# Pooled attention and two feed-forward blocks on one core: one more pair of heads with its queries on partitions, column sums as two more columns, other ranks

## The chip, the cores and the metric

One core of a Trainium2 chip runs the whole program: TensorE (matrix products), VectorE, ScalarE, GpSimd, and SyncE, which here only issues DMAs. The metric is the time of one execution on the device in microseconds, the median of several runs. A profile is taken of one further execution.

## The reference

All arrays are float32. There are 4 batches of 8 heads, 1152 positions and 64 columns a head.

```python
q_pool = q.reshape(B, H, S // 2, 2, D).mean(axis=3)          # 576 queries a head
scores = matmul(q_pool, k.T) / sqrt(D)                       # 576 x 1152
scores = scores - max(scores, axis=-1)
attn = exp(scores); attn = attn / (sum(attn, axis=-1) + 1e-09)
x = heads side by side of matmul(attn, v)                    # 2304 x 512
h = maximum(x @ w_in, 0); g = s * (h * h) + b                # 2304 x 2048
y = g @ w_out                                                # 2304 x 512
gate = sigmoid(y @ w_gate); val = y @ w_val                  # 2304 x 1536
out = (gate * val) @ w_out2                                  # 2304 x 512
```

The weights are 64-bit floats that the kernel turns into 32-bit ones itself. In the first feed-forward block the shift `b` of `g` adds `b` times the column sums of `w_out` to `y`; the kernel computes these sums once, in batch 0's pass, and keeps them as a bias.

## The kernel before

**Number format.** A 32-bit operand is split into a high part in TensorE's fast 32-bit format and a low part, the remainder. A product of two such operands is three matmuls (high by high, high by low, low by high: `mm3`, L530 to L536, its matmuls on L532 to L534). Every split costs a cast (`copy_sb`, on ScalarE or GpSimd) and a subtraction (`tt_sb`, on VectorE or GpSimd, whichever the plan chooses).

**Attention.** Work goes by pairs of heads, four pairs a batch. `pair_prep` loads q, k and v, adds neighbouring queries, and transposes q and k by TensorE. Two forms of the rest exist.

- Keys on partitions (`pair_half`, batches 1 to 3): for each head and each half of the queries (288), nine blocks of 128 keys give scores with keys on partitions (two matmuls of 288 columns each, L762). ScalarE copies each block out of PSUM, VectorE keeps a running maximum over the blocks (L469), TensorE transposes it (L775), VectorE reduces it (L779), TensorE spreads it back to all partitions (L740), VectorE subtracts it (three tiles of 864 columns), ScalarE takes the exponential (L788), the result is split, and three P·V matmuls of 288 columns a block follow (L810, L811, L815). A column of ones beside V gives the sums; their reciprocal is taken either by a round trip through DRAM (`inverse`) or, where the pair ends a batch, directly (L859).
- Queries on partitions (`pair_rows`, batch 0): a block of 128 queries (eight full ones, and one that holds the last 64 of both heads) gets its scores in three PSUM banks of 384 keys (L893). VectorE takes the maximum along the row (L900, L903), and ScalarE the exponential straight out of PSUM with the maximum as bias, the row's sum falling out beside it (L907). P is then transposed by TensorE, 128 x 128 at a time (L938, and L940 for the half block), copied and split, and multiplied with V (L960). The transposed P has its high and low part in a `g` tile, which batch 0's attention shares with the feed-forward pass that follows.

**First feed-forward block** (`ffn1`, once a batch): `x` is split, 16 tiles of hidden columns are computed ("up", two halves of 288 tokens), squared, split into a `g` tile (high part, low part), and every four of them are multiplied with `w_out` ("down") into four output tiles. In batch 0, ahead of the second half of each output tile, eight matmuls of two columns (L623: two high and low weight tiles by four hidden tiles, against a tile of ones) add up the column sums of `w_out`. Batch 0's pass also decodes the weights (L490 to L500) and stores them to DRAM; later passes fetch them back. The pass of a batch needs `x` of all four pairs; it runs beside the next batch's attention.

**Second feed-forward block** (`ffn2`): twice, each for two batches, after all attention; batch 3's first pass stands between.

**What sets the order.** The kernel records every operation with its engine (or two to choose from), an estimated duration, what it reads and writes, and a rank; `Plan.order` then plays these through time, and at each step starts on every free engine the ready operation of lowest rank (class of work, plus an offset per name from `MOVED`, then position in the program, with a second offset). The order that results is written into each engine's queue and stays fixed. Tiles and PSUM banks are handed out by the same play, with the numbers in `ROOM`: 8 banks in all; at most 8 for tag `pr` (batch 0's attention), 4 for `ps` (the other batches'), 6 for `ff`; six `pp` tiles and four `g` tiles.

The operations of "down" and the column sums:

```python
py = bank(fp)
for i in range(CH):
    mm3(f"{fp} down", lambda py=py: py.t[:, :HQ], HQ, ...)
if b == hf == 0:
    def column_sums(py=py, w2=w2, ds_=ds_):
        for i in range(CH):
            for w in range(2):
                nc.tensor.matmul(py.t[:, HQ:HQ + 2], lhsT=w2[i].t[:, w, ds_], rhs=ones2, ...)
```

Of the kernel before, what the change touches and what calls it, by code (L numbers as in the profile page):

```python
# [32 lines left out]
DIRECT = (1, 2)  # L33
BANKS = {"pr", "ps", "pm", "acc", "ff", "p2"}
# [4 lines left out]
    "q load": (32, -5),  # L39
    "k load": (33.5, 3),  # L40
    "v load": (45.5, -117),
    "v hi": (-38, -97),
    "v lo": (2, -108),
    "q add": (0, -82),
    "q twice": (19, 27),
    "pr qT": (0, 101),
    "pr q hi False": (5, -93),
    "pr q lo False": (20, 103),
    "pr q hi True": (12, 120),
    "pr q lo True": (-8, -119),  # L50
    "pr kT": (-18.5, -55),
    "pr k hi": (-5, -44),
    "pr k lo": (-10, -71),
    "s b load": (30, -129),
    "r qk 1": (0, 189),
    "r max": (33.5, -59),
    "r - max": (-40, 91),
    "r exp": (57, -26),
    "r pT": (-40, 55),
    "r p": (-4.5, 57),  # L60
    "r p hi": (1, -106),
    "r p lo": (-40, -100),
    "r pv": (-40, -109),
    "r pT hi": (0, 83),
    "r pT lo": (36.5, 15),
    "r o": (-40, -167),
    "r x add": (35.5, -40),
    "r qk 2": (-17.5, 92),
    "r sums": (-34, 21),
    "r sums eps": (3.5, 149),  # L70
    "r 1 / sums": (0, -9),
    "r spread": (-40, -44),
    "r rows": (0, -88),
    "r rows mid": (0, 279),
    "r x / sums": (-1.5, -118),
    "r x / sums mid": (52, -15),
    "r end": (0, 96),
    "ps qT": (2, -29),
    "ps q hi False": (60, 90),
    "ps q lo False": (-37, -29),  # L80
    "ps kT": (-37.5, 16),
    "ps k hi": (23.5, 77),
    "ps k lo": (0, 7),
    "xx hi": (38, -89),
    "xx lo": (0, 93),
    "w load": (-1, -143),
    "w top": (-18.5, 97),
    "w scale": (-8, 23),
    "w low": (-19, 3),
    "w join": (11, 15),  # L90
    "w sign": (-36.5, 3),
    "w hi": (-40, 67),
    "w lo": (-40, 124),
    "w keep": (1, -49),
    "ff xx up": (59, 10),
    "ff relu": (-16, -95),
    "square": (-2.5, -142),
    "g hi": (7.5, 83),
    "g lo": (0, -7),
    "ff down": (52.5, 72),  # L100
    "column sums": (60, 35),
    "column sum": (30, 111),
    "ff y": (5, 96),
    "ff y add": (16.5, -46),
    "bias": (-10, -34),
    "y bias": (60, 105),
    "y store": (-21, -30),
    "qk": (33, -11),
    "s copy": (21, 43),
    "s max": (14, 112),  # L110
    "max T": (29, -81),
    "max": (60, 64),
    "max rows": (24.5, -22),
    "s - max": (16, 71),
    "exp": (1, 151),
    "p hi": (-40, 84),
    "p lo": (6.5, -89),
    "pv hi": (15, -72),
    "pv lo": (36, -18),
    "sums": (31.5, -144),  # L120
    "x": (44, 118),
    "sums out": (1, -73),
    "sums in": (3, 38),
    "1 / sums spread": (6.5, 129),
    "1 / sums out": (56, 107),
    "1 / sums in": (22, -4),
    "x / sums": (0, 61),
    "1 / sums": (46.5, -68),
    "w fetch": (-5.5, 3),
    "w come": (-40, 82),  # L130
    "x store": (28, 26),
    "yy load": (35.5, -43),
    "yy hi": (-5.5, -14),
    "yy lo": (0, 48),
    "p2 yy up": (51, -50),
    "gate": (22, 37),
    "gate val": (-40, 130),
    "h hi": (-4.5, -101),
    "h lo": (-36.5, 79),
    "down 2": (-16, -101),  # L140
    "out": (0.5, 5),
    "out add": (1.5, -9),
    "out store": (0, 9),
    "xx load": (1.5, -33),
    "p2 xx up": (23, -29),
    "p2 relu": (8, -42),
    "p2 down": (33.5, 24),
    "p2 y": (1.5, 110),
    "p2 y add": (60, 59),
# [196 lines left out]
def kernel(  # L346
# [47 lines left out]
    ones = const.tile([P, 1], F32, name="ones")  # L394
    nc.gpsimd.memset(ones, 1.0)
    zero = const.tile([P, 1], F32, name="zero")
    nc.gpsimd.memset(zero, 0.0)
# [3 lines left out]
    eps = const.tile([P, 1], F32, name="eps")  # L401
    nc.gpsimd.memset(eps, 1e-9)
    ones2 = const.tile([P, 2], F32R, name="ones2")
    nc.vector.tensor_copy(out=ones2, in_=ones.to_broadcast([P, 2]))
# [3 lines left out]
    s_sb = const.tile([P, 1], F32, name="s_sb")  # L408
# [169 lines left out]
    def ffn1(b, xx):  # L578
# [7 lines left out]
        for f0 in range(0, F1, CH):  # L586
            g = []
            for f in range(f0, f0 + CH):
# [4 lines left out]
                if b == B - 1 and f % 2:  # L593
                    gg = slot("fh", "h", [P, 2, 2 * SQ], F32R, lambda t: t[:, :, :SQ])
                else:
                    gg = slot("fg", "g", [P, 2, SQ], F32R)
# [7 lines left out]
                split_g(gg, lambda gg=gg: gg.t[:, 0], lambda gg=gg: gg.t[:, 1], lambda r=r: r.t, SQ, both, (gg, 0), (gg, 1))  # L604
                g.append(gg)
            w2 = [h for f in range(f0, f0 + CH, 2) for h in load_w((w_out, rows, "1d", f), (w_out, rows, "1d", f + 1))]
            for d in range(KC):
                ds_ = slice(d * P, (d + 1) * P)
                for hf in range(2):
                    cs = slice(hf * HQ, (hf + 1) * HQ)  # L610
                    py = bank(fp)
                    for i in range(CH):
                        mm3(
                            f"{fp} down", lambda py=py: py.t[:, :HQ], HQ,
                            lambda i=i, w2=w2, ds_=ds_: w2[i].t[:, 0, ds_], lambda i=i, w2=w2, ds_=ds_: w2[i].t[:, 1, ds_],
                            lambda i=i, g=g, cs=cs: g[i].t[:, 0, cs], lambda i=i, g=g, cs=cs: g[i].t[:, 1, cs],
                            [py, *((s, w) for s in (*w2, *g) for w in range(2))], i == 0, i == CH - 1, [y],
                        )
                    if b == hf == 0:
                        def column_sums(py=py, w2=w2, ds_=ds_):  # L620
                            for i in range(CH):
                                for w in range(2):
                                    nc.tensor.matmul(py.t[:, HQ:HQ + 2], lhsT=w2[i].t[:, w, ds_], rhs=ones2,  # L623
                                                     start=(i == w == 0), stop=(i == CH - 1 and w == 1))

                        pe("column sums", 2 * CH * mm(2), column_sums, [(s, w) for s in w2 for w in range(2)], [py], FP)
# [6 lines left out]
                    if f0 == 0:  # L633
                        act(f"{fp} y", HQ + 112, lambda d=d, cs=cs, py=py: nc.scalar.activation(  # L634
# [504 lines left out]
```

## Time and profile before

| | |
|---|---|
| runs | 1453.57, 1455.32, 1452.1 us (median 1453.57) |
| the profiled execution | 1461.99 us, its span 1460.2 us, mean granted TensorE clock 0.988 |
| TensorE busy | 1395.9 us (96%), 9292 matmuls |
| VectorE busy | 1076.8 us (74%) |
| ScalarE busy | 944.8 us (65%) |
| GpSimd busy | 763.7 us (52%) |
| column sums (L623) | 128 matmuls |
| HBM | 114 GB/s over the span |

The span reaches from the first to the last instruction; the execution's own time is a little longer. Matmuls overlap in the trace, so the duration of one is longer than its share of TensorE's time: two starts in a row tell the share. Batch 0's attention ends at 192 us, batch 1's at 460, batch 3's at 843, and from there on only feed-forward work is left. A granted clock of 1.00 is 2.4 GHz, and one of 0.5 is 1.2 GHz; a mean in between says how much of a stretch was at either.

### The profile page before, as it was taken

The page shows a single profiled execution, that of the slowest core. Times are in us where ns is not written, and L with a number is a line of the kernel's source. Part 1 is how long each engine was busy: PE and PEld are TensorE (multiplying, and loading weights), DVE is VectorE, ACT ScalarE, POOL GpSimd, SP SyncE. Part 2 cuts the span into 40 slices and gives each one's busy share as a digit, 9 for nine tenths or more (in the row PEclk, how much of TensorE's full clock was granted, in tenths as well). Part 3 has the DMA queues.
Part 4 walks back from the last instruction along what each step waited for, and adds up shares of the span by engine and source line. Part 5 has one row for each costly group of instructions (what it writes and reads, how often), then busy time and mean ns, then how long its engine had stood idle before and what let it go on. Part 6 is the DMA issues. An engine that isn't in the chain of part 4 may idle for free. (4 is left out here: it accounts for less than half of the span.)

```text
span 1460.2 us, 25288 instructions
## 1 busy us (share of the span) xinstructions
PE 1395.9 (96%) x9292; PEld 1332.2 (91%) x9292; DVE 1076.8 (74%) x1775; ACT 944.8 (65%) x2008; POOL 763.7 (52%) x650
## 2 busy tenths in 40 slices
PE   7988999998999999999999999999999999999998
PEld 6877889898889999999999999999898999989897
DVE  6889898998988888989999746737485126838562
ACT  6889888878788999898899735434142534534240
POOL 3677566778777565565766534525253003625230
PEclk9999999999999999999999999999999999999999
DMA  3335133444540533234241373312236544313112
GB/s 90 93 114 191 38 98 99 142 147 138 175 159 14 201 107 105 82 111 132 74 145 46 108 272 130 101 58 87 73 100 208 184 173 142 119 45 127 36 68 65
DMA packets 103044, 167.90 MB, mean 115 GB/s; under 512 B 44652, under 2 KB 80264, under 8 KB 93832
## 3 DMA queue, kind: packets, MB, share of 16 engines
q1 hardware_dynamic: 96008, 115.95, 25.5%
q0 software_dynamic: 6912, 50.33, 9.6%
q8 instruction: 73, 1.20, 0.3%
q14 instruction: 51, 0.42, 0.1%
HBM read 139.99 MB, written 26.28 MB: 114 GB/s over the span
## 5 line engine op out<-in xcount | busy, mean ns | idle before, releaser
L466 POOL TENSOR_TENSOR pp<-st,pp 128x864 fp32r<-128x864 f32 x94 | 202.5, 2161 | 33.8 <-ACT pp L456 27.8
L534 PE MATMUL banks<-yy,w 128*128 128x384 f32 x576 | 192.6, 334 | 0.3 <-POOL w L466 0.3
L533 PE MATMUL banks<-yy,w 128*128 128x384 f32 x576 | 192.6, 334 | 0.1
L532 PE MATMUL banks<-yy,w 128*128 128x384 f32 x576 | 192.5, 334 | 0.0
L463 ACT COPY st<-banks 128x288 f32<-128x288 f32 x432 | 153.9, 408 | 47.9 <-PE banks L762 43.6
L762 PE MATMUL banks<-qT,kT 128*128 128x288 f32 x864 | 165.7, 307 | 3.6 <-DVE mx L469 2.5
L469 DVE TENSOR_TENSOR mx<-banks,mx 128x288 f32<-128x288 f32 x336 | 150.6, 449 | 15.6 <-ACT st L463 8.1
L532 PE MATMUL banks<-xx,w 128*128 128x288 f32 x512 | 153.5, 300 | 5.0 <-DMA w<-d_1u_1u 5.0
L469 DVE TENSOR_TENSOR st<-st,banks 128x864 f32<-128x864 f32 x144 | 149.7, 1044 | 3.8 <-PE banks L740 3.0
L534 PE MATMUL banks<-xx,w 128*128 128x288 f32 x512 | 151.8, 296 | 0.0
L533 PE MATMUL banks<-xx,w 128*128 128x288 f32 x512 | 151.7, 296 | 0.0
L490 POOL TENSOR_SCALAR raw<-raw 128x512 f32<-128x512 f32 x99 | 78.4, 792 | 129.1 <-DMA raw<-in_moe_w_gate_dram 40.9
L532 PE MATMUL banks<-g,w 128*128 128x288 f32 x448 | 137.0, 306 | 0.9 <-ACT xy L634 0.6
L788 ACT ACTIVATE st<-st 128x864 f32<-128x864 f32 x144 | 132.7, 929 | 6.4 <-DVE st L469 5.8
L762 PEld LDWEIGHTS banks<-qT,kT 128*128 128x128 f32 x864 | 128.7, 191 | 8.2 <-DVE mx L469 5.3
L533 PE MATMUL banks<-g,w 128*128 128x288 f32 x448 | 133.1, 297 | 0.0
L534 PE MATMUL banks<-g,w 128*128 128x288 f32 x448 | 133.1, 297 | 0.0
L810 PE MATMUL banks<-pp,vt 128*128 128x288 f32 x432 | 122.3, 303 | 10.6 <-ACT pp L456 7.9
L493 ACT ACTIVATE raw<-raw 128x512 f32<-128x512 f32 x104 | 71.2, 686 | 79.5 <-POOL raw L490 73.3
L811 PE MATMUL banks<-pp,vt 128*64 128x288 f32 x432 | 119.5, 296 | 0.0
L466 POOL TENSOR_TENSOR w<-raw,w 128x512 fp32r<-128x512 f32 x64 | 100.3, 1569 | 19.8 <-ACT w L456 18.6
L494 DVE TENSOR_SCALAR raw<-raw 128x512 uint32<-128x512 uint32 x104 | 74.1, 715 | 47.2 <-DMA raw<-in_moe_w_val_dram 18.3
(151 smaller groups left out, 4016.5 us busy)
## 6 DMA issues: line engine op xcount, KB each, us to landing
w<-d_1u_1u POOLq DMA_DIRECT2D x24, 1024.0 KB, 6.2
w<-d_1d_1d POOLq DMA_DIRECT2D x24, 1024.0 KB, 6.2
raw<-in_moe_w_out_dram SPq DMA_DIRECT2D x40, 512.0 KB, 4.1
raw<-in_moe_w_gate_dram SPq DMA_DIRECT2D x24, 512.0 KB, 4.5
raw<-in_moe_w_val_dram SPq DMA_DIRECT2D x24, 512.0 KB, 3.9
qn<-in_q_dram SPq DMA_DIRECT2D x16, 576.0 KB, 4.2
kn<-in_k_dram SPq DMA_DIRECT2D x32, 288.0 KB, 4.4
vn<-in_v_dram SPq DMA_DIRECT2D x32, 288.0 KB, 2.9
```

What stands on the lines that cost most here:

```text
L463: act(name, n, lambda: nc.scalar.copy(out=out(), in_=in_()), r, w, rank, sbuf=False)
L466: shared(name, n, lambda e: ENGINE[e].tensor_tensor(out=out(), in0=in0(), in1=in1(), op=op), r, w, rank, 2.15)
L469: dve(name, n, lambda: nc.vector.tensor_tensor(out=out(), in0=in0(), in1=in1(), op=op), r, w, rank)
L490: shared("w top", 512, lambda e: ENGINE[e].tensor_scalar(out=words(1).bitcast(F32), in0=words(1).bitcast(F32), scalar1=F64_TOP, scalar2=-F ...
L494: dve("w low", 512, lambda: nc.vector.tensor_scalar(out=words(0), in0=words(0), scalar1=29, scalar2=None, op0=ALU.logical_shift_right,), [ ...
L532: nc.tensor.matmul(ps(), lhsT=whi(), rhs=xhi(), start=first, stop=False)
L533: nc.tensor.matmul(ps(), lhsT=whi(), rhs=xlo(), start=False, stop=False)
L534: nc.tensor.matmul(ps(), lhsT=wlo(), rhs=xhi(), start=False, stop=last)
L762: nc.tensor.matmul(ps.t[:, :HQ], lhsT=kT.t[:, c], rhs=qq[:, w, hf * HQ:(hf + 1) * HQ], start=(w == 0), stop=(w == 1))
L788: act("exp", 3 * HQ, lambda s=s: nc.scalar.activation(out=s.t, in_=s.t, func=AF.Exp), [], parts, AT)
L810: nc.tensor.matmul(acc.t[:, :HQ], lhsT=vt.t[:, 3 * i + c, D:], rhs=hi.t[:, c], start=(i == c == 0), stop=False)
L811: nc.tensor.matmul(acc.t[:D, :HQ], lhsT=vt.t[:, 3 * i + c, :D], rhs=hi.t[:, c], start=False, stop=False)
```

## The change

- Pair 3 of batch 1 is computed with queries on partitions, in the form that batch 0 has. Its PSUM banks come from the tag `ps`, and its transposed P from `pp` tiles, two to a unit, in place of a `g` tile. Its names begin with `t` and `pt` and so have ranks of their own.
- The column sums are no matmuls of their own. A `g` tile is 32 columns longer and holds its low part first, then the high part, then two columns of ones, which GpSimd writes each time in batch 0's pass ("one"). In the second half's products the two matmuls with the high part of `g` are 290 columns wide in place of 288, so the sums of the weights' high and low parts arrive beside the result.
- The constants share one tile, the tile of ones for the column sums goes, and one small tile is padded to 128 bytes.
- All offsets in `MOVED` are replaced.

```diff
+ROWS = {(0, hp) for hp in range(4)} | {(1, 3)}
 MOVED = {
...
 }
...
-    s_sb = const.tile([P, 1], F32, name="s_sb")
+    s_sb = const.tile([P, 32], F32, name="s_sb")[:, :1]
...
+    def g_slot():
+        return slot("fg", "g", [P, 2 * SQ + 32], F32R)
+    def part(gg, w):
+        return gg.t[:, :SQ] if w else gg.t[:, SQ:]
...
-    def mm3(name, ps, n, whi, wlo, xhi, xlo, reads, first, last, to):
+    def mm3(name, ps, n, whi, wlo, xhi, xlo, reads, first, last, to, ps_lo=None):
         def issue():
             nc.tensor.matmul(ps(), lhsT=whi(), rhs=xhi(), start=first, stop=False)
-            nc.tensor.matmul(ps(), lhsT=whi(), rhs=xlo(), start=False, stop=False)
+            nc.tensor.matmul((ps_lo or ps)(), lhsT=whi(), rhs=xlo(), start=False, stop=False)
             nc.tensor.matmul(ps(), lhsT=wlo(), rhs=xhi(), start=False, stop=last)
...
-                    gg = slot("fg", "g", [P, 2, SQ], F32R)
+                    gg = g_slot()
+                if b == 0:
+                    plan.add("one", "POOL", 150, lambda gg=gg: nc.gpsimd.tensor_scalar(
+                        out=gg.t[:, 2 * SQ:2 * SQ + 2], in0=ones.to_broadcast([P, 2]), scalar1=1.0, scalar2=0.0, op0=ALU.mult, op1=ALU.add),
+                             [], [(gg, "one")], FE)
...
+                    n = HQ + 2 if b == 0 and hf else HQ
+                    cs, ch = slice(hf * HQ, hf * HQ + n), slice(hf * HQ, (hf + 1) * HQ)
                     py = bank(fp)
                     for i in range(CH):
                         mm3(
-                            f"{fp} down", lambda py=py: py.t[:, :HQ], HQ,
+                            f"{fp} down", lambda py=py, n=n: py.t[:, :n], n,
...
-                    if b == hf == 0:
-                        def column_sums(py=py, w2=w2, ds_=ds_):
-                            for i in range(CH):
-                                for w in range(2):
-                                    nc.tensor.matmul(py.t[:, HQ:HQ + 2], lhsT=w2[i].t[:, w, ds_], rhs=ones2,
-                                                     start=(i == w == 0), stop=(i == CH - 1 and w == 1))
...
-        by_rows = b == 0
-        tag = "pr" if by_rows else "ps"
+        by_rows = (b, hp) in ROWS
+        tag = "pr" if b == 0 else "ps"
...
-    def pair_rows(hp, prep, x):
+    def pair_rows(b, hp, prep, x):
...
+        def parts2():
+            if b == 0:
+                t = g_slot()
+                return [(t, (t, w), lambda w=w: part(t, w)) for w in range(2)]
+            return [(t, t, lambda t=t: t.t) for t in (slot("pp", "pp", [P, 3 * HQ], F32R) for w in range(2))]
...
-        if b == 0:
-            steps = pair_rows(hp, prep, x0)
+        rows_now = (b, hp) in ROWS
+        if rows_now:
+            steps = pair_rows(b, hp, prep, xs[b])
             next(steps)
         else:
             pair_half(b, hp, 0, prep)
```

## Rows read from the trace of the kernel before

**Rows 1.** Stages: us; busy us (instructions) by engine; TensorE clock, DMA share, GB/s.
```profile
0.00:192.00 192.00, 165.25 (x1110) 149.26 (x1111) 158.80 (x353) 160.66 (x459) 117.44 (x138) 0.96 0.35 106
192.00:460.00 268.00, 249.04 (x1822) 239.86 (x1822) 241.18 (x398) 225.83 (x456) 197.06 (x136) 0.97 0.40 128
460.00:843.00 383.00, 374.74 (x2813) 363.33 (x2812) 334.56 (x551) 337.56 (x697) 230.44 (x169) 1.00 0.34 109
843.00:1460.20 617.20, 606.91 (x3554) 579.77 (x3552) 342.26 (x475) 220.72 (x397) 218.75 (x208) 0.99 0.35 116
```

**Rows 2.** TensorE's waits, 192 to 480 us: total us, times, longest.
```profile
PE banks L810 <- ACT pp L456: 6.4, 3, 3.9
PE banks L740 <- DVE mc L779: 3.4, 3, 2.0
```

**Rows 3.** Timeline of TensorE around one burst: start, us, instruction.
```profile
239.85 0.95 PE L623 MATMUL banks<-ones,w 128*128 128x2 f32 x8
240.66 0.38 PE L532 MATMUL banks<-g,w 128*128 128x288 f32 x1
240.88 0.30 PE L533 MATMUL banks<-g,w 128*128 128x288 f32 x1
```

**Rows 4.** Full stretches: 384-column matmuls alone, then 288-column ones (columns of rows 1).
```profile
1060.00:1080.00 20.00, 20.00 (x117) 20.00 (x116) 19.12 (x23) 9.19 (x17) 13.35 (x11) 1.00 0.32 101
1180.00:1200.00 20.00, 20.00 (x153) 20.00 (x152) 6.08 (x11) 5.93 (x11) 2.12 (x4) 1.00 0.60 211
```

**Rows 5.** Timeline of TensorE in a batch-0 pair (queries on partitions).
```profile
36.95 0.77 PE L960 MATMUL banks<-g,vt 128*128 128x320 f32 x4
37.56 0.38 PE L938 MATMUL banks<-ident,st 128*128 128x128 f32 x2
37.77 0.33 PE L940 MATMUL banks<-ident,st 128*128 128x64 f32 x2
37.95 0.39 PE L938 MATMUL banks<-ident,st 128*128 128x128 f32 x2
```

**Rows 6.** VectorE's groups by form: count | busy us, mean ns | idle before.
```profile
L469 DVE TENSOR_TENSOR mx<-banks,mx 128x288 f32<-128x288 f32 x336 | 150.6, 449 | 15.6 <-ACT st L463 8.1 <-PE banks L740 0.5
L469 DVE TENSOR_TENSOR st<-st,banks 128x864 f32<-128x864 f32 x144 | 149.7, 1044 | 3.8 <-PE banks L740 3.0 <-ACT st L463 0.7
L466 DVE TENSOR_TENSOR pp<-st,pp 128x864 fp32r<-128x864 f32 x50 | 66.3, 1327 | 13.2 <-ACT pp L456 12.2 <-POOL pp L458 0.9
L900 DVE TENSOR_REDUCE sg<-banks 128x1 f32<-128x384 f32 x108 | 56.4, 550 | 11.6 <-PE banks L893 11.0
L469 DVE TENSOR_TENSOR g<-banks,g 128x320 fp32r<-128x320 f32 x36 | 17.2, 482 | 4.2 <-ACT g L463 4.0
```

**Rows 7.** ScalarE's groups by form, the same columns.
```profile
L463 ACT COPY st<-banks 128x288 f32<-128x288 f32 x432 | 153.9, 408 | 47.9 <-PE banks L762 43.6 <-DVE mx L469 1.9 <-POOL xx L466 0.3
L788 ACT ACTIVATE st<-st 128x864 f32<-128x864 f32 x144 | 132.7, 929 | 6.4 <-DVE st L469 5.8
L907 ACT ACTIVATE st<-banks,sg 128x384 f32<-128x384 f32 x108 | 62.8, 597 | 10.0 <-DVE sg L903 9.8
L907 ACT ACTIVATION_READ_ACCUMULATOR st<-banks,sg 128x1 f32 x108 | 23.5, 218 | 0.0
```

**Rows 8.** A stretch with a lower mean clock (columns of rows 1).
```profile
340.00:360.00 20.00, 15.35 (x97) 14.77 (x96) 16.69 (x27) 17.55 (x32) 17.74 (x12) 0.83 0.46 163
```

**Rows 9.** Timelines of VectorE and GpSimd: x divided by its sums, where pairs end.
```profile
113.74 0.22 DVE L469 TENSOR_TENSOR xy<-xy,banks 64x64 f32<-64x64 f32 x1
163.52 0.44 DVE L469 TENSOR_TENSOR xy<-xy,banks 64x64 f32<-64x64 f32 x2
192.33 0.23 DVE L469 TENSOR_TENSOR xy<-xy,banks 64x64 f32<-64x64 f32 x1
421.81 0.80 POOL L466 TENSOR_TENSOR xy<-xy,rr 128x288 f32<-128x288 f32 x1
459.73 0.65 DVE L466 TENSOR_TENSOR xy<-xy,s 128x288 f32<-128x288 f32 x1
```

More of the change, by code (lines that the diff above doesn't have):

```diff
@@ L57 @@
[L57 to L149, printed above, removed]
+    "q load": (5, -16),
+    "k load": (33.5, 8),
+    "v load": (49, -85),
+    "v hi": (0, -33),
@@ new lines @@
+    "v lo": (60, 95),
+    "q add": (60, 14),
+    "pr qT": (0, -183),
+    "pr q hi False": (12.5, -90),
+    "pr q lo False": (-2, -114),
+    "pr q hi True": (20.5, -2),
+    "pr q lo True": (40.5, 49),
+    "pr kT": (-15, -30),
+    "pr k hi": (0, 74),
+    "pr k lo": (-24, -95),
+    "s b load": (0, 61),
+    "r qk 1": (0, 18),
+    "r max": (21, 114),
+    "r - max": (-27, 50),
+    "r exp": (30, 52),
+    "r pT": (-31.5, 90),
+    "r p": (-19.5, -22),
+    "r p hi": (0, 81),
+    "r p lo": (-2, -12),
@@ new lines @@
+    "r pv": (-40, -101),
+    "r pT hi": (0, -44),
+    "r pT lo": (47.5, 168),
+    "r o": (-11.5, -132),
+    "r x add": (32, -65),
+    "r qk 2": (-17.5, 0),
+    "r sums": (36, -32),
+    "r sums eps": (5, -38),
+    "r 1 / sums": (-30, -140),
+    "r spread": (-0.5, 78),
+    "r rows": (-12.5, 121),
+    "r rows mid": (0, 87),
+    "r x / sums": (-0.5, -61),
+    "r x / sums mid": (58, -115),
+    "r end": (1.5, -70),
+    "ps qT": (58.5, -62),
+    "ps q hi False": (46.5, 117),
+    "ps q lo False": (0, 49),
@@ new lines @@
+    "ps kT": (13, 8),
+    "ps k hi": (20, 44),
+    "ps k lo": (-4.5, 84),
+    "xx hi": (17, 66),
+    "xx lo": (56, -103),
+    "w load": (-17, -11),
+    "w top": (0, -72),
+    "w scale": (0, -38),
+    "w low": (-15, -53),
+    "w join": (4.5, -116),
+    "w sign": (-15, -93),
+    "w hi": (-40, 198),
+    "w lo": (-22.5, -114),
+    "w keep": (-8.5, -14),
+    "one": (-40, -113),
+    "ff xx up": (60, 22),
+    "ff relu": (-7.5, 64),
+    "square": (-7.5, 68),
+    "g hi": (2.5, 51),
+    "g lo": (0, 60),
@@ new lines @@
+    "ff down": (60, -8),
+    "ff y": (25, 46),
+    "column sum": (0, 119),
+    "ff y add": (12.5, 121),
+    "bias": (23.5, 47),
+    "y bias": (21, 39),
+    "y store": (-6, 1),
+    "qk": (26, -103),
+    "s copy": (12.5, -50),
+    "s max": (8.5, -24),
+    "max T": (25, -25),
+    "max": (22, -112),
+    "max rows": (0, 155),
+    "s - max": (12.5, 86),
+    "exp": (0, -79),
+    "p hi": (-29.5, -83),
+    "p lo": (0, -90),
+    "pv hi": (14.5, 75),
+    "pv lo": (55, 225),
+    "sums": (40.5, -43),
@@ new lines @@
+    "x": (25, 31),
+    "sums out": (-2, -94),
+    "sums in": (-13, 111),
+    "1 / sums spread": (0, -73),
+    "1 / sums out": (55, -125),
+    "1 / sums in": (-5, -53),
+    "x / sums": (0, 105),
+    "pt qT": (47, -118),
+    "pt q hi False": (0, 95),
+    "pt q lo False": (0.5, -49),
+    "pt q hi True": (-40, -60),
+    "pt q lo True": (-2, -74),
+    "pt kT": (-40, -90),
+    "pt k hi": (22.5, 106),
+    "pt k lo": (60, 47),
+    "t qk 1": (35, 2),
+    "t max": (25, 108),
+    "t - max": (0, 108),
@@ new lines @@
+    "t exp": (60, 115),
+    "t pT": (-14, 99),
+    "t p": (-16.5, 34),
+    "t p hi": (0, 106),
+    "t p lo": (0, -115),
+    "t pv": (-40, -142),
+    "t pT hi": (-40, 58),
+    "t pT lo": (32.5, 116),
+    "t o": (0, -43),
+    "t x add": (0, -19),
+    "t qk 2": (-13, -21),
+    "t sums": (0, -124),
+    "t sums eps": (-6.5, 95),
+    "t 1 / sums": (3, -34),
+    "t spread": (0, 48),
+    "t rows": (-34, 50),
+    "t rows mid": (-0.5, 20),
+    "t x / sums": (5, -88),
+    "t x / sums mid": (10, 20),
@@ new lines @@
+    "t end": (-5, 28),
+    "w fetch": (-32.5, -85),
+    "w come": (2, -29),
+    "1 / sums": (57, 6),
+    "x store": (-10, 37),
+    "turn": (0, 51),
+    "yy load": (0, -89),
+    "yy hi": (0, -25),
+    "yy lo": (1, -20),
+    "p2 yy up": (30.5, 31),
+    "gate": (5, 73),
+    "gate val": (-40, 106),
+    "h hi": (25.5, 79),
+    "h lo": (-40, -79),
+    "down 2": (-40, 1),
+    "out": (17, -42),
+    "out add": (-12.5, 20),
+    "out store": (-40, 28),
+    "xx load": (-14.5, 30),
+    "p2 xx up": (-3, 20),
@@ L150 @@
+    "p2 relu": (0, 109),
+    "p2 down": (12.5, 8),
+    "p2 y": (49.5, -42),
+    "p2 y add": (35.5, 68),
 }
@@ L393 @@
     make_identity(nc, ident)
[L394 to L397, printed above, removed]
+    values = const.tile([P, 3], F32, name="values")
+    ones, zero, eps = (values[:, i:i + 1] for i in range(3))
+    for t, value in ((ones, 1.0), (zero, 0.0), (eps, 1e-9)):
+        nc.gpsimd.memset(t, value)
     qm = const.tile([P, 2, 2, P], F32R, name="qm")
     nc.vector.tensor_copy(out=qm.rearrange("p j w c -> p (j w c)"), in_=zero.to_broadcast([P, 4 * P]))
[L401 to L404, printed above, removed]
     sums2 = const.tile([P, KC], F32, name="sums2")
     bias = const.tile([P, KC], F32, name="bias")
-    s_sb = const.tile([P, 1], F32, name="s_sb")
+    s_sb = const.tile([P, 32], F32, name="s_sb")[:, :1]
     b_sb = const.tile([P, 1], F32, name="b_sb")
```

117 lines of the change are left out of this document (51 added, 66 removed).

## The prediction

> **What bounds the kernel now.** I read the busy time of each engine by stage first [rows 1]. From 843 us to the end TensorE is busy 606.9 of 617.2 us and VectorE idles nearly half of the time: only fewer TensorE instructions shorten that part, and the change removes none there. In batches 2 and 3 (460 to 843 us) TensorE is busy 374.7 of 383. In batch 1 (192 to 460 us), where nearly all that the change removes and adds lies, three engines are close together: TensorE 249.0 of 268, VectorE 241.2 (90%), ScalarE 225.8 (84%), GpSimd 197.1. TensorE is first there, but 19 us of the stage it stands still, and the list of its waits, read second, names ScalarE and VectorE as the longest releasers, in front of a P·V product and of the transposed maxima [rows 2]. Batch 0 (up to 192 us) has no feed-forward work to fill with and lets TensorE idle 26.8 us.
>
> So a TensorE microsecond removed in batch 1 is worth close to a microsecond, provided that VectorE and ScalarE don't fall due instead; and the start and the seams depend on the order alone.
>
> **The change part by part.** Column sums. The timeline of TensorE shows a burst of eight two-column matmuls [rows 3]: the first starts at 239.85, the next operation at 240.66, so 0.81 us; that operation then takes 0.22 us to its successor, where a 288-column matmul takes 0.131 (153 in 20 us of full work [rows 4]), so 0.90 us counted to there. There are 4 blocks of 4 hidden tiles by 4 output tiles, 16 bursts: 13.0 to 14.4 us. I take 13.7. What is added: 64 products of half 1, in each two matmuls wider by 2 columns, 256 columns. From 0.171 us at 384 columns and 0.131 at 288 [rows 4] a column costs 0.42 ns: 0.1 us. Net -13.6 us on TensorE.
>
> Of this burst the Trainium skill would say otherwise: "TensorE: Matmul & The Clock Gate", section "Back-to-back issue gap", gives 1 to 64 columns about 60 cycles, 25 ns. By that rule 128 of them are an estimated 3.2 us, and the whole change would add TensorE work. The trace disagrees: eight in 0.81 us are 101 ns each. The same page's section on LDWEIGHTS gives a load of 128 columns 107 ns, which the trace supports; no run here shows which of the two sets the pace.
>
> The sixteen new two-column writes stand on GpSimd, which has 71 us free in batch 1 [rows 1]; they depend on nothing but a free tile. I count nothing. If the cover were gone, the second half of a "down" product would wait for its tile's write, behind one long GpSimd operation at most, and with it all that follows on TensorE. Wider or padded tiles (g by 128 bytes, s_sb to 128) I take at nothing too: g was 36 times 128 bytes and is 37 times; no row of the trace tells start addresses apart.
>
> The moved pair, on TensorE. Keys on partitions, as now: 72 score matmuls and 108 P·V matmuls of 288 columns, 180 x 0.131 = 23.6 us, and 24 transposes for the maxima, at most at the 0.105 us of a full-width one (two from 37.56 to 37.77 [rows 5]), 2.5: 26.1 us. Queries on partitions: 60 score matmuls of 384 columns, 60 x 0.171 = 10.3; 72 transposes of P at 0.105, 7.6; 36 half-width ones at 0.09 (two from 37.77 to 37.95 [rows 5]), 3.2; 36 P·V of 320 columns at 0.152 (four from 36.95 to 37.56 [rows 5]), 5.5; 36 of 256 columns at 0.131 - 32 x 0.42 ns = 0.118, 4.2; five for the sums, 0.5. Sum 31.3 us: the pair costs TensorE 5.2 us more (4 to 7 with the scatter of these pitches).
>
> On VectorE the same pair: now 32 x 0.449 for running maxima, 12 x 1.044 for subtracting them, and its share of the low parts, 12 x 50/144 x 1.327: 14.4 + 12.5 + 5.5 = 32.4 us. Then 27 x 0.550 and half of 10,368 columns of low parts at 482 ns per 320: 14.9 + 7.8 = 22.7 us [rows 6]. That is 9.7 less, 4% of its batch-1 load; the small rest (reciprocals, reductions, the halves' sum) is alike. On ScalarE: now 36 x 0.408 + 12 x 0.929 = 25.8 us of copies and exponentials; then 27 x (0.597 + 0.218) = 22.0 [rows 7], but half of P's columns are then copied out of PSUM before they are cast. I take ScalarE as unchanged, give or take 3 us. The division's trip through DRAM for this pair's first half goes; it isn't what TensorE waits for in [rows 2].
>
> Stalls. TensorE's waits for VectorE's maxima and for casts of P in [rows 2] are of a kind that this pair no longer has; it gets those of batch 0 (scores waiting for a PSUM bank until the exponential has read it), with four banks in place of eight. With feed-forward products as filler I put the net at -1 us; the sides are -5 and +3. One long wait costs more than itself: in 340 to 360 us, where 3.9 us of [rows 2] fall, the granted clock is 0.83 [rows 8], that is a third of the stretch at 1.2 in place of 2.4 GHz, some 3.4 us of work not done.
>
> The order. Every name's rank is replaced, so every queue is shuffled: SP's loads, GpSimd's weight fetches and the compute engines. The trace of before has no row for that. What can be won or lost is TensorE's idle time, 26.8 + 19.0 + 8.3 + 10.3 us [rows 1]; a third of the first two is 15 us. Either sign is open: 0, with 15 us on both sides and 6 as the usual size.
>
> Sum: -13.6 + 5.2 - 1 + 0 = -9.4 us. The profiled execution of before took 1461.99 us, 1.8 above its span; with the change 1452.6. The median of the runs stands 8.4 below the profiled execution (1453.57), so the forecast is 1444.2 us.
>
> **The rivals.** (a) The other side: the moved pair ends later, and TensorE starves. The next feed-forward pass needs all four pairs. Now pair 2 ends at 421.81 (plus 0.8) and pair 3 at 459.73 (plus 0.65), 38 us later [rows 9]; in batch 0 pairs in the new form end 49.8 and 28.8 us after one another (113.74, 163.52, 192.33 [rows 9]), there with eight banks and four more buffers for the transposed P, which this pair hasn't. If it takes 50 us, the next pass comes 12 us later, with nothing but one block's "down" products to fill; TensorE loses these 12 us and some 3.4 at the lower clock, against 9.4 won: +6, 1459.6 us. It decides from 47 us on (38 + 9.4). Against it: 28.8 us was possible, and in batch 0 the other engines had weights to decode at the same time.
>
> (b) TensorE's relief is not cashed. If batch 1 goes at the pace of ScalarE, which the change leaves as it is, removed matmuls only lengthen TensorE's waits. For it: the longest waits in [rows 2] are for ScalarE's casts. Against it: ScalarE has 42 us idle there, VectorE 27. Time 1453, between 1450.7 and 1456.4.
>
> (c) The order gains as well: 8 us of batch 0's 26.8 idle on top of the sum, 1436 us, down to 1428. For it: that stage's idle is the largest of all. Against it: there is no filler in it, and its first microseconds are waits for data.
>
> (d) Two-column matmuls cost little by themselves, and other work would fill the same slots. At 25 ns each, far below the row, 3.2 us go and 5.2 come, with the stall's -1: +1, 1454.6 us; it is the result by the rule of the Trainium skill named above, and the row of the burst speaks against it.
>
> **How the numbers follow.** Forecast 0.56 (its own range 1438 to 1450.5: the bounds of the pair and the stalls, and 6 us for the order), (a) 0.12, (b) 0.13, (c) 0.17, (d) 0.02. What this kernel's measurement can tell from no change is 0.2%, 2.9 us. Faster: forecast and (c), 0.73. Same: (b) and (d), 0.15. Slower: (a), 0.12. The range 1430 to 1457 takes in the forecast, (b), (d) and most of (c), and leaves out the far end of (c) and most of (a), somewhat under 0.2.
>
> **What would show it.** Right: no two-column matmuls by themselves; TensorE's busy time down by about 8 us, all of it between 192 and 480 us; VectorE down by 8 to 10; the division that closes batch 1, at 459.7 us now, 8 to 10 us earlier, and the rest shifted with it. (a) is seen in an x that closes batch 1 after 460 us and a TensorE wait ahead of the next pass's first product; (b) in a batch 1 as long as now with more waits for ScalarE; (c) in a batch 0 that ends before 185 us. I would be wrong if batch 1 shrank by much less than the removed matmuls, or if the new order opened waits after 843 us, where the old one has 10.3 us in all.

## The result and the profile after

The changed kernel takes 1475.57 us (median, 1471.25 to 1477.15) against 1454.44 for the one before beside it: ratio 1.0134 [1.0116, 1.0153] over the runs taken beside each other (the two medians alone would give 1.0145), so 1.3% slower, not 0.6% faster. Its profiled execution took 1474.67 us, its span 1472.9.

The stages, with the columns of [rows 1]:

```profile
0.00:192.00 192.00, 164.59 (x1113) 150.01 (x1114) 159.39 (x354) 160.80 (x461) 119.03 (x143) 0.96 0.36 107
192.00:460.00 268.00, 243.24 (x1732) 230.81 (x1731) 239.58 (x407) 221.25 (x478) 188.93 (x154) 0.97 0.42 137
460.00:843.00 383.00, 368.66 (x2751) 355.46 (x2751) 334.44 (x546) 336.07 (x698) 235.05 (x168) 1.00 0.30 98
843.00:1472.90 629.90, 615.53 (x3615) 588.34 (x3613) 344.35 (x478) 220.82 (x398) 225.12 (x212) 0.99 0.36 116
```

TensorE does have less to do: 9205 matmuls in place of 9292, and with each counted at the median step, from a start to the next one, of its line and form in the same trace, 1332.3 us in place of 1340.6. That is 8.3 us less, where the sum had 13.6 - 5.2 = 8.4. What grew is its idle time: in 192 to 460 us from 19.0 [rows 1] to 24.8, in 460 to 843 from 8.3 to 14.3, afterwards from 10.3 to 14.4. (A second profile of the kernel before, below, has 16.8, 8.3 and 8.6.) No burst of two columns is left, and the wider products are there (groups of TensorE by form):

```profile
L570 PE MATMUL banks<-g,w 128*128 128x290 f32 x64 | 19.8, 310 | 0.3 <-DVE kT L507 0.3
L572 PE MATMUL banks<-g,w 128*128 128x290 f32 x64 | 19.0, 296 | 0.0
```

Batch 0 ends as before, batch 1 two us later rather than nine earlier (VectorE's timeline, answering [rows 9]):

```profile
191.65 0.23 DVE L507 TENSOR_TENSOR xy<-xy,banks 64x64 f32<-64x64 f32 x1
...
461.70 0.23 DVE L507 TENSOR_TENSOR xy<-xy,banks 64x64 f32<-64x64 f32 x1
```

TensorE's waits from 192 to 480 us: the one for ScalarE's casts of P has shrunk from 6.4 us [rows 2] to 1.4, and several others stand in its place.

```profile
PE banks L780 <- DVE mc L819: 5.5, 5, 1.9
PE banks L815 <- DVE mx L507: 3.1, 3, 2.1
PE banks L855 <- POOL pp L504: 2.8, 3, 1.7
PE banks L1009 <- DVE pp L507: 2.2, 3, 1.5
PE banks L850 <- ACT pp L494: 1.4, 4, 0.5
```

VectorE's groups by form, answering [rows 6]. The pair's own saving is here: -12.4, -13.1 and -7.9 us in the first three rows, +13.5 in the fourth, +4.3 in the fifth and +3.1 in two more shapes of it, -12.5 in all. Yet VectorE's total went from 1076.8 to 1077.8 us: under the new order it took single operations that GpSimd had before (three additions of queries, and the like), and some operations took longer each (five of `x<-x,s` 1532 ns on the mean, where four took 934).

```profile
L507 DVE TENSOR_TENSOR mx<-banks,mx 128x288 f32<-128x288 f32 x308 | 138.2, 450 | 21.1 <-ACT st L501 11.5 <-PE banks L802 0.3
L507 DVE TENSOR_TENSOR st<-st,banks 128x864 f32<-128x864 f32 x132 | 136.6, 1042 | 2.6 <-PE banks L780 2.5
L504 DVE TENSOR_TENSOR pp<-st,pp 128x864 fp32r<-128x864 f32 x46 | 58.4, 1271 | 11.1 <-ACT pp L494 9.6 <-POOL pp L496 1.3
L942 DVE TENSOR_REDUCE sg<-banks 128x1 f32<-128x384 f32 x135 | 69.9, 549 | 13.6 <-PE banks L935 13.1
L507 DVE TENSOR_TENSOR pp<-banks,pp 128x320 fp32r<-128x320 f32 x9 | 4.3, 481 | 0.4 <-ACT pp L501 0.3
```

And the time behind the attention, where nothing was removed or added, is part of the loss. SyncE stores the last `x` of the attention at 842.9 us, and from there to the end of the span it takes 630.0 us; before it took 623.8 and, in a second profile of that kernel, 620.3. (There the last `x` is stored at 836.4 and 835.7 us, some 7 us ahead of the 843 at which [rows 1] is cut.)

### The profile page after: what moved, and what is told of

Read it like the earlier page. It is cut to its first block, busy times and chain, and to the rows that moved or that the text cites. A ratio compares the mean times of both kernels' runs of the same rounds, so it can differ in the third digit from the quotient of the medians.

```text
span 1472.9 us, 25105 instructions
## 1 busy us (share of the span) xinstructions
PE 1392.0 (95%) x9205; PEld 1324.6 (90%) x9205; DVE 1077.8 (73%) x1783; ACT 938.9 (64%) x2033; POOL 768.1 (52%) x675
## 4 chain that ended last, share of the span: by engine, by line
PE 60%; ACT 16%; DVE 10%; DMA 6%; issue 5%; POOL 2%; SPq 0%; DVEq 0%; ACTq 0%; POOLq 0%
PE banks L570 12%; PE banks L572 12%; PE banks L571 12%; PE banks L802 3%; ACT st L828 3%; ACT st L501 3%; PE banks L1090 3%; PE banks L1091 3%; PE banks L1089 3%; ACT pp L494 2%; DVE mx L507 2%; PE banks L935 2%; PE banks L1009 2%; PE banks L850 2%; PE banks L855 2%
## 5 line engine op out<-in xcount | busy, mean ns | idle before, releaser
L504 POOL TENSOR_TENSOR pp<-st,pp 128x864 fp32r<-128x864 f32 x86 | 185.5, 2165 | 39.8 <-ACT pp L494 31.7
L501 ACT COPY st<-banks 128x288 f32<-128x288 f32 x396 | 139.5, 410 | 37.3 <-PE banks L802 22.3
L507 DVE TENSOR_TENSOR mx<-banks,mx 128x288 f32<-128x288 f32 x308 | 138.2, 450 | 21.1 <-ACT st L501 11.5
L802 PE MATMUL banks<-qT,kT 128*128 128x288 f32 x792 | 145.0, 302 | 2.7 <-DVE mx L507 2.1
L507 DVE TENSOR_TENSOR st<-st,banks 128x864 f32<-128x864 f32 x132 | 136.6, 1042 | 2.6 <-PE banks L780 2.5
L828 ACT ACTIVATE st<-st 128x864 f32<-128x864 f32 x132 | 121.1, 929 | 8.6 <-DVE st L507 7.7
L802 PEld LDWEIGHTS banks<-qT,kT 128*128 128x128 f32 x792 | 115.5, 188 | 6.1 <-DVE mx L507 4.5
L850 PE MATMUL banks<-pp,vt 128*128 128x288 f32 x396 | 112.9, 305 | 6.2 <-ACT pp L494 3.6
L851 PE MATMUL banks<-pp,vt 128*64 128x288 f32 x396 | 109.6, 297 | 0.0
L571 PEld LDWEIGHTS banks<-yy,w 128*128 128x128 f32 x576 | 108.1, 188 | 1.5 <-POOL yy L504 1.2
L570 PEld LDWEIGHTS banks<-yy,w 128*128 128x128 f32 x576 | 108.1, 188 | 0.3
```

The costliest lines, as they stand in the source:

```text
L501: act(name, n, lambda: nc.scalar.copy(out=out(), in_=in_()), r, w, rank, sbuf=False)
L504: shared(name, n, lambda e: ENGINE[e].tensor_tensor(out=out(), in0=in0(), in1=in1(), op=op), r, w, rank, 2.15)
L507: dve(name, n, lambda: nc.vector.tensor_tensor(out=out(), in0=in0(), in1=in1(), op=op), r, w, rank)
L571: nc.tensor.matmul((ps_lo or ps)(), lhsT=whi(), rhs=xlo(), start=False, stop=False)
L802: nc.tensor.matmul(ps.t[:, :HQ], lhsT=kT.t[:, c], rhs=qq[:, w, hf * HQ:(hf + 1) * HQ], start=(w == 0), stop=(w == 1))
L828: act("exp", 3 * HQ, lambda s=s: nc.scalar.activation(out=s.t, in_=s.t, func=AF.Exp), [], parts, AT)
```

## The experiments

Each ratio is to the kernel before, on the same chip, with its 95% interval. "Ranks" are the numbers in `MOVED`. Two theories stood against each other from the start: that the loss comes with the order (the ranks, and the play that they are put through), or that it comes with what is computed (the pair above all).

### The column sums alone, in the order of before

Half 0 of the queries is put behind half 1 in a `g` tile, so that the two columns of ones stand beside the half that has the bursts. The burst is an empty operation in the plan; every queue keeps before's order, and GpSimd has 16 two-column writes more.

```diff
-                        def column_sums(py=py, w2=w2, ds_=ds_):
...
-                        pe("column sums", 2 * CH * mm(2), column_sums, [...], [py], FP)
+                        pe("column sums", 2 * CH * mm(2), lambda: None, [...], [py], FP)
```

> The kernel before with the column sums as two more columns and nothing else: every queue of VectorE, ScalarE and SyncE stands in the order of before, TensorE's too but for the bursts that are gone, and GpSimd has sixteen two-column writes more. Theory O (the removed TensorE time is worth nearly its length where the order stays; the loss of the change lies in its order): 9 to 14 us faster than before, 1440 to 1445. Rival B (batch 1 goes at the pace of VectorE and ScalarE, the removed matmuls only lengthen TensorE's waits): within 3 us of before, and the end of batch 1's attention at 459 us as it was.

1451.59 us, ratio 0.9969 [0.995, 0.9988]: the only kernel here that beats the one before, and the changed one by 1.6%. But of 13.6 us of TensorE some 4 came back (2 to 7 by the interval), between the two expectations. Before was profiled a second time for this. The ends of batches 0 and 1 (VectorE's timeline) in that second profile:

```profile
191.30 0.23 DVE L469 TENSOR_TENSOR xy<-xy,banks 64x64 f32<-64x64 f32 x1
...
458.77 0.64 DVE L466 TENSOR_TENSOR xy<-xy,s 128x288 f32<-128x288 f32 x1
```

and with the columns alone:

```profile
189.43 0.22 DVE L472 TENSOR_TENSOR xy<-xy,banks 64x64 f32<-64x64 f32 x1
...
452.10 0.64 DVE L469 TENSOR_TENSOR xy<-xy,s 128x288 f32<-128x288 f32 x1
```

Batch 1 takes 262.7 us in place of 267.5: 4.8 less. The other 1.9 us were gained in batch 0, ahead of the first burst, with a granted clock of 0.98 in place of 0.96, so they are no relief of the bursts. From the end of batch 0 to the end of batch 1 TensorE is busy 239.6 us in place of 251.3 and idle 23.7 in place of 16.8: 11.6 us less work, of which 6.8 turned into waits. The two longest waits are the old ones, a little longer; the product of the low part of P waits 2.3 us more for GpSimd, and the rest is spread over many small waits (TensorE in 192 to 460 us, in the second profile of before and then with the columns alone, whose line numbers are 5 higher):

```profile
PE banks L810 <- ACT pp L456: 6.7, 3, 3.9
PE banks L762 <- DVE mx L469: 2.5, 4, 1.1
PE banks L815 <- POOL pp L466: 0.2, 1, 0.2
```

```profile
PE banks L815 <- ACT pp L459: 7.3, 4, 3.9
PE banks L767 <- DVE mx L472: 3.0, 6, 0.8
PE banks L820 <- POOL pp L469: 2.5, 4, 1.6
```

> The kernel before, profiled once more. The profiled execution on which the prediction rests lies 8 us above the median of the runs. If that excess sits in one place (the seams at 862 and 1118 us, where TensorE waits for weights from DRAM), this profile is shorter there and equal up to 843 us; if it is spread, every stage is a little shorter. Its own time 1452 to 1460 us.

1457.73 us, span 1456.0. Up to 843 us the two profiles of before agree to a microsecond; the first one's other 3 us lie in the seams behind that, some 2 at 860 to 880 us and 1 at 1130 to 1150.

### Each burst issued twice

```diff
+                            for _ in range(2):
-                            for i in range(CH):
+                                for i in range(CH):
...
```

> The kernel before, every queue in its order, with each burst of eight two-column matmuls issued twice: 13.0 to 14.4 us more TensorE work. If TensorE's time in batch 1 counts in full, 12 to 15 us slower than before. If the stage has slack on TensorE, as the kernel with the bursts gone suggests (4 us won of some 13.6), 3 to 7 us slower.

1477.93 us, ratio 1.0162 [1.0142, 1.0182]: 23 us for twice 128 matmuls in place of 128, more than either expectation. Batch 1 now takes from 187.47 to 476.60 us, 21.6 more than before. From start to start a matmul of the doubled bursts takes 127 ns on the mean. The stage from 192 to 460 us, of before and then of this kernel, with the columns of [rows 1]:

```profile
192.00:460.00 268.00, 251.19 (x1824) 242.64 (x1824) 239.20 (x398) 224.70 (x454) 196.90 (x136) 0.96 0.40 128
```

```profile
192.00:460.00 268.00, 254.42 (x1794) 246.46 (x1793) 221.18 (x363) 209.22 (x420) 182.16 (x127) 0.91 0.39 126
```

The mean granted clock is 0.91 in place of 0.96: 18% of the stretch at 1.2 GHz in place of 9%, so some 12 us of full-speed work lost (from the unrounded means). It isn't chance of one profile: over whole executions the four runs of this kernel have 0.981 to 0.983, the 14 of before beside them 0.989 to 0.996. The queues are those of before, so no order can make up the difference; the clock's 12 us and the bursts' own 13 to 14 [rows 3] are somewhat more than the 21.6 (part of the bursts ran at the lower clock). Why the clock falls with them isn't shown.

This answers rival (d), two-column matmuls that cost little by themselves. The 4 us won by taking the bursts away would fit it, but added bursts are not cheap, and TensorE's work fell by 11.6 us above, not by 3.2. The figure that the prediction took for it, an estimated 3.2 us for 128 ("TensorE: Matmul & The Clock Gate" of the Trainium skill, section "Back-to-back issue gap"), is given there for a single matmul by itself, and the section says that it leaves out the weight load at small sizes; the prediction left that out. Here every matmul of a burst has a weight load of its own, and 101 to 127 ns from one to the next agree with the section's warning. Taking bursts away doesn't mirror adding them: +23 us there, -4 here.

### Structure and ranks, crossed

Ranks of before for the changed structure (the names `t` and `pt` take those of `r` and `pr`), ranks of after for the old one, and each part alone: the columns with either set, the pair with before's only. For the columns alone one line takes the moved pair out again; for the pair alone the bursts are put back.

```diff
-ROWS = {(0, hp) for hp in range(4)} | {(1, 3)}
+ROWS = {(0, hp) for hp in range(4)}
```

> The changed kernel with the ranks of before (the moved pair's names take the ranks of batch 0's names). Theory O: the order of the new ranks costs, so this is clearly faster than the changed kernel, 1455 to 1466, though these ranks were not made for it. Rival S (the moved pair or the columns cost the time, under any ranks): 1470 to 1485.

> The kernel before with the ranks of the changed kernel, where a name exists in both. Theory O: slower than before by 15 us or more, 1468 to 1485. Rival S: within 5 us of before.

> The kernel before with the changed kernel's column sums and the ranks of before, so that the order is played anew (no moved pair). The same work as in the kernel that kept every queue of before (1451.6 us), in another order. Theory O: an order that these ranks were not chosen for costs some 10 us: 1458 to 1468. Rival: orders from like ranks are alike, 1448 to 1455.

> The changed kernel without the moved pair: the column sums as columns, the new ranks. Theory S: faster than the changed kernel, 1455 to 1468, since the pair is what costs. Theory O: slower than it, 1476 to 1490, since the ranks were made for the pair (before's work under these ranks took 1487.7).

> The kernel before with the moved pair alone, the ranks of before, the order played anew. Theory S (the moved pair itself costs): no faster than both parts under these ranks (1469.1) by more than what the columns give, 1472 to 1480. Theory O (any order played anew under these ranks costs about the same, the pair little): 1460 to 1470.

| ranks | before's form | columns alone | pair alone | both |
|---|---|---|---|---|
| of before | 1 | 1.0073 [1.0051, 1.0095] | 1.0166 [1.014, 1.0191] | 1.0102 [1.0074, 1.0129] |
| of after | 1.0228 [1.0196, 1.0261] | 1.0159 [1.0137, 1.018] | not run | 1.0134 [1.0116, 1.0153] |

Each set does best with the form that it stands with, though for the ranks of after by less than the intervals (1.0134 against 1.0159). Most times fall where theory O put them or just beside it: 1467.93 us for the columns alone with before's ranks, 1479.96 with after's, 1487.7 for before's form with after's ranks. But both parts with before's ranks take 1469.09, between the two expectations, and the pair alone 1482.15, more than either. Columns alone with before's ranks do the same products as the first experiment, with the halves and the constants laid out otherwise, but in another order, since taking out an operation lets the plan start others elsewhere; the ratio goes from 0.9969 to 1.0073. So some 15 us come with the shuffle that a small removal sets off; the other layout isn't tried by itself. This is what the prediction's "0, with 15 us on both sides" had no row for.

### More orders

Four more sets of ranks, two for the columns alone and two for both parts, each searched for its own structure by playing the plan with other offsets; and the kernel before with 50 of 111 offsets changed.

```diff
-    "q load": (32, -5),
-    "k load": (33.5, 3),
+    "q load": (34, 3.0081),
+    "k load": (35.5, -36.3814),
...
```

> The kernel before with 50 of its 111 names' ranks changed, so that a fifth of TensorE's neighbours in its queue are others, and the planner's play is as long as before to 0.2%. If orders that the planner rates alike are alike on the chip: within 4 us of before. If the planner can't tell them apart: 5 to 20 us slower.

> The changed kernel (moved pair, columns) under a third set of ranks, which a random search made from the ranks of before, in the planner's play of this very kernel. Theory O (the loss lies in the new ranks' order): 1452 to 1465. Rival S (this structure costs under any ranks): 1468 to 1480.

> The columns alone (no moved pair), under ranks that the same search made for it. Theory O: as good as a fitted order, 1448 to 1460. If even ranks searched for leave 1464 or more, the planner's play isn't a guide to the chip within 1%, and the order of before is a lucky one.

> The whole change with a fourth set of ranks, found by a search that started elsewhere than the third. Theory O (only the order costs, the moved pair itself nothing): the two orders of the whole change scatter as much as those without the pair, and this one may come out anywhere from 1450 to 1480 us, at the mean of all orders no higher than the columns alone. Theory S (the moved pair costs some 1% under any order): 1468 to 1480 us, and 10 to 18 us above the columns alone with their fourth ranks.

> The column sums alone, the pair left as it was, with ranks from another search than the third. Theory O: 1448 to 1475 us, not clearly below the whole change with its fourth ranks. Theory S: 1450 to 1462 us, 10 to 18 us below the whole change with its fourth ranks.

Before with near ranks: 1.0063 [1.0039, 1.0087], by order alone. In the first two rows of the next table both kernels have the same ranks and differ in the moved pair and what the plan makes of it. In the last two every one of the 144 ranks differs between them, so these rows hold two unlike orders as well. "Last x" is where SyncE stores the last x of the attention, "then" the time from there to the end of the span, both from one profile each:

| ranks | columns alone: ratio, last x, then | both: ratio, last x, then |
|---|---|---|
| of before | 1.0073, 835.9, 631.0 | 1.0102, 842.3, 625.5 |
| of after | 1.0159, 839.1, 638.1 | 1.0134, 842.9, 630.0 |
| third, one set each | 1.0006 [0.999, 1.0021], 837.0, 619.4 | 1.0131 [1.0109, 1.0152], 843.2, 628.9 |
| fourth, one set each | 1.0028 [1.001, 1.0047], 833.2, 622.8 | 1.009 [1.0063, 1.0117], 835.3, 632.4 |

The moved pair brings last x later in every row, by 6.4, 3.8, 6.2 and 2.1 us, 4.6 on the mean. These are single profiles, and two of the same queues can differ by nearly 4 us there (842.9 in the changed kernel, 839.2 in the last one below). In the whole time it costs +0.29, -0.25, +1.25 and +0.62%, 0.48% or 7 us on the mean, with a scatter of 0.6%, so a mean good to 0.3% and not clear of nothing: the scatter comes from "then", where neither kernel has a pair left and the differences are -5.5, -8.1, +9.5 and +9.6 us. Up to last x the pair's cost is of the size of its TensorE time. In the whole time its cost isn't settled: by their times (1473.31 and 1468.94 us) both kernels with the third and fourth sets fall where theory S put them, but under equal ranks the pair costs about nothing. The pair at a held order wasn't run.

Columns alone, at four orders, leave last x at 833.2 to 839.1 us, where before has 835.7 to 836.4; only the held order brings it to 828.6 (then 619.1).

### The seam at 1110 us

At about 1110 us the second block's first half ends, and batch 3's first pass and the reload of batch 2's `y` (`yl`) set the next work. After, SyncE's timeline:

```profile
1107.16 0.37 SPq L523 DMA_DIRECT2D raw<-in_moe_w_gate_dram  x1
1107.58 0.50 SPq L690 DMA_DIRECT2D y_d<-xy  x1
1110.60 16.26 SPq L1104 DMA_DIRECT2D out_dram<-fo  x6
1126.96 0.53 SPq L581 DMA_DIRECT2D yl<-y_d  x1
```

and VectorE's:

```profile
1120.23 0.43 DVE L532 TENSOR_SCALAR raw<-raw 128x512 uint32<-128x512 uint32 x1 [9.66 <-DMA raw<-in_moe_w_gate_dram]
...
1123.75 2.48 DVE L507 TENSOR_TENSOR fo<-banks,fo 128x512 f32<-128x512 f32 x4
```

A raw weight tile is some 13 us on its way; VectorE waits 9.7 us to decode it; the additions that make the output tiles `fo` stand behind that in VectorE's queue; six output DMAs wait for `fo` in SyncE's queue; `yl` stands behind them; GpSimd waits 12.4 us for `yl`, and its next weight fetch stands behind that. In the end TensorE waits 7.9 us for that fetch, and the granted clock is 0.80 in 1135 to 1160 us, where before it was 1.00. In that stretch TensorE idles 5.7 us more than before and loses 5 us of full-speed work to the clock: together the size of what was lost behind the attention.

The kernel before has the same pieces, and its raw tile is as long on its way, but `yl` goes out 14.6 us after the store of `y`, not 19.4, and GpSimd's next fetch at 1130.0 us, not 1138.7 (SyncE's timeline of before):

```profile
1103.57 0.50 SPq L652 DMA_DIRECT2D y_d<-xy  x1
1104.31 0.37 SPq L485 DMA_DIRECT2D raw<-in_moe_w_gate_dram  x1
1108.44 9.69 SPq L1055 DMA_DIRECT2D out_dram<-fo  x8
1118.18 0.59 SPq L543 DMA_DIRECT2D yl<-y_d  x1
```

Two cures were tried. One lets that reload wait for the first quarter of batch 3's pass, so that weight fetches go ahead of it on GpSimd:

```diff
+                if b == B - 1 and f0 == 0 and d == KC - 1:
+                    plan.add("late", "END", 0, lambda: None, [(y, KC - 1, 1)], ["late"], FE)
...
-            load_split("fy", "yy", y_d[b0 + b], [("y_d", b0 + b)], gate, ...)
+            load_split("fy", "yy", y_d[b0 + b], [("y_d", b0 + b), *(["late"] if b0 else [])], gate, ...)
```

> The changed kernel, with one dependency more: the last y that is loaded back (batch 2's, for the second feed-forward block's second half) waits for the first quarter of batch 3's pass, so that GpSimd's queue has its weight fetches ahead of the splits that wait for this load. Nothing before 1100 us changes. Theory O: the 7.9 us wait of TensorE for a weight tile at 1143 us in the changed kernel goes, and the low clock behind it: 7 to 10 us faster than the changed kernel, 1465 to 1469. Rival: the weights land late anyway, since the stores of the output hold the DMA engines; then within 2 us of the changed kernel.

1470.89 us, ratio 1.0109 [1.0082, 1.0136]: 0.25% below the changed kernel, less than expected, and with intervals that overlap, so no gain is shown; the fetch now goes out at 1136 us, but it takes some ten to land. The other moves a single DMA in the finished order, the load of `yl`, to right behind the store that it reads:

```diff
+        i = self.early[EARLY]
+        old = out.index(i)
+        mine = {(s.tag, s.k) for s in ops[i][5]}
+        at = max(p for p, u in enumerate(out[:old])
+                 if u in ops[i][4] or mine & {(s.tag, s.k) for s in ops[u][5]}) + 1
+        out.insert(at, out.pop(old))
         return out
```

> The changed kernel with one DMA moved in SyncE's queue alone: the load of batch 2's y (yl) is issued right behind the store of that y, ahead of the six output stores that the profile after shows between them (yl at 1126.96 us, the store of y at 1107.58). All other queues keep their order. If the loss after 843 us comes from the place of this load, TensorE's idle time of 8.4 us more than before in 1110 to 1165 us goes: 1466 to 1469 us, ratio 1.008 to 1.010. If the weight's raw tile that lands 13 us after its issue, with VectorE standing behind its decoding, sets the seam whatever SyncE does, nothing or at most 2 us is won: 1473 to 1476 us.

1468.39 us, ratio 1.0082 [1.0067, 1.0097]: 0.52% won, some 7.5 us, by the place of one transfer. SyncE's timeline and the stretch 1135 to 1160 us, of this kernel and then, for the stretch, of after and before:

```profile
1104.34 0.50 SPq L701 DMA_DIRECT2D y_d<-xy  x1
1118.69 0.34 SPq L592 DMA_DIRECT2D yl<-y_d  x1
1119.07 10.91 SPq L1115 DMA_DIRECT2D out_dram<-fo  x13
```

```profile
1135.00:1160.00 25.00, 20.65 (x145) 20.45 (x144) 4.41 (x6) 12.38 (x25) 1.58 (x3) 0.93 0.55 198
```

```profile
1135.00:1160.00 25.00, 17.00 (x103) 16.35 (x103) 7.84 (x11) 10.38 (x21) 5.89 (x6) 0.80 0.61 211
```

```profile
1135.00:1160.00 25.00, 22.72 (x172) 22.52 (x172) 5.31 (x7) 14.15 (x28) 1.59 (x3) 1.00 0.62 223
```

The load goes out 14.4 us after the store, which it still has to wait for; TensorE's wait is down to 4.3 us. TensorE's matmuls stand in the same order in both kernels, so their profiles can be set against each other matmul by matmul: this one is 3.2 us ahead at 1119 us, where nothing differs yet, and 8.6 at 1174, so the seam itself gave 5.4. Its share of the loss is shown; the rest of the seam is not undone.

## Why the prediction was wrong

By steps, against the four that it added up. The stages of three profiles, cut where batches 0 and 1 end and where the last x is stored, in us, with TensorE's idle time in brackets:

| | batch 0 | batch 1 | batches 2 and 3 | from last x on |
|---|---|---|---|---|
| before, second profile | 191.3 (26.1) | 268.1 (16.8) | 376.3 (8.3) | 620.3 (8.6) |
| columns alone, order held | 189.4 (25.5) | 263.3 (23.7) | 375.9 (8.4) | 619.1 (8.0) |
| changed | 191.7 (27.4) | 270.2 (24.8) | 381.0 (14.3) | 630.0 (14.4) |

Each row is one profile, and two profiles of the same queues differ by up to some 4 us over the span. The medians put the changed kernel 21 us behind before, the ratio 19.5, and these two spans 16.9.

- **Columns: -13.6 us predicted, -4 measured** at the held order (-4.8 in batch 1, by one profile each). The work was sized rightly; the step that failed is "a TensorE microsecond removed in batch 1 is worth close to a microsecond". At the same order more than half of the relief became idle time. This is rival (b) in its outcome, and it had 0.13; the wait that it named, for ScalarE's casts, grew by 0.6 us only, those for VectorE's maxima and GpSimd's low parts by more.
- **Moved pair: +5.2 predicted.** In batch 1 the changed kernel takes 6.9 us more than the columns alone at the held order, 5.8 of them TensorE's busy time; the mean of four orders at last x is +4.6. The size is right as far as these profiles reach. Rival (a)'s loss didn't come: batch 1's x does close after 460 us, at 461.7, but no wait stands ahead of the next pass, and TensorE's longest between 455 and 480 us is 2.1 us.
- **Stalls: -1 predicted, with sides of -5 and +3; in batch 1 they grew by 8.0.** Of this 6.8 stand in the columns alone too: it is mostly their relief that wasn't cashed, not the pair. Waits for casts went, waits for maxima and low parts came; VectorE's saving, right in size, was spent by the order.
- **Order: 0, usually 6, at most 15; in fact some 16 to 19.** This is what failed by most. Against the columns alone at the held order the changed kernel loses 25.2 us by the profiles: 2.3 in batch 0 (of the size of the scatter), 6.9 in batch 1 (the pair, and 1.1 of waits), 5.1 in batches 2 and 3 and 10.9 from last x on. The last two, 16, are the order's, for next to nothing was removed or added there; the medians, 24 us apart, leave 17 to 19 beside the pair. The bound of 15 was a third of the idle time of the first two stages; the loss came in the two stages that had 8 us of idle time each, as new waits (6 us in each) and as lower clock at the seam. The prediction had only a remark that new waits behind 843 us would make it wrong. Of that part the place of one load is 5.4 us by the profiles and 7.5 by the ratios. Rival (c) didn't come: batch 0 ends at 191.7 us.

One reading beside the sum needs care: the prediction's "107 ns, which the trace supports" is the distance between the weight loads of a burst (some 114 ns); their records last 187 ns and more.

The symmetric guess was the other error behind that size. Twelve kernels here were played anew, the changed one among them, and not one was faster than before: one was equal, one 0.3% slower, and ten slower by 0.6 to 2.3%, whichever part of the change they had. Around this order a shuffle was no coin with two sides; its usual cost in these runs is some 15 us, the pair's in it where it was moved.

What stays open: which changed ranks made the waits in batches 2 and 3, why the order of before is better than its neighbours, and whether an order exists at which the moved pair gains.

## What to carry to other kernels

A number that comes out of removing work holds for the order in which it was read. If the edit also makes a planner play the whole program anew, first make the edit with every queue held as it was; here that was worth 15 us and gave the only version that won. Where four engines are 73 to 94% busy, as in this batch 1, a microsecond taken off the busiest was worth a third of one. Don't take the idle time of the old order as the bound of what another order can lose: here the loss came where there was least of it. And look at the places behind the edit where one late transfer holds three queues in a row.

## What the runs showed of the hardware that was not expected

- Adding 128 two-column matmuls, 13 to 16 us by their steps, cost 23 us and took the mean granted clock of 192 to 460 us from 0.96 to 0.91 (of the whole execution to 0.981 to 0.983, where the runs of before have 0.989 to 0.996); taking 128 away gave 4.
- A store of 1152 KB on SyncE landed 7.0 us after its issue in the profile of before at the seam, with one raw weight load issued 0.4 us ahead of it and one 0.7 us behind; in the last kernel the load that needs it went out 14.4 us after it, behind raw weight loads issued 0.4 and 1.6 us ahead of the store. Moving a load ahead in its queue gains no more than its source's landing allows.
